# One operation and four small transfers for a head's hash bits, the product with the values in two runs, and a new order of the whole plan

## The chip, the cores and the metric

The kernel runs on one core of a Trainium2 chip. The metric is device time in microseconds (us), the median of the runs. TensorE (PE) multiplies matrices, VectorE (DVE), ScalarE (ACT) and GpSimd (POOL) work element by element, SyncE (SP) issues the transfers (DMAs). Each engine takes its instructions strictly in the order in which they stand in its own program, and waits on semaphores for what others make. SBUF is the on-chip memory, PSUM the memory that TensorE writes its sums to.

## The reference

Sixteen heads (2 batches of 8) of attention with 768 rows and 64 columns, masked by a hash, then two wide layers over 1536 tokens:

```python
q_bits = (np.einsum('bhsd,dk->bhsk', q, proj) > 0).astype(np.int64)   # 6 bits of a row
k_bits = (np.einsum('bhsd,dk->bhsk', k, proj) > 0).astype(np.int64)
mask = q_bucket[:, :, :, None] == k_bucket[:, :, None, :]             # all 6 bits alike
scores = np.where(mask, scale * np.matmul(q, k.transpose(0, 1, 3, 2)), -1e9)
attn = softmax(scores); x = np.matmul(attn, v)                        # heads side by side: 1536 x 512
h = x @ w_in1; x = (np.maximum(h, 0) + alpha * np.minimum(h, 0)) @ w_out1   # 512 -> 2048 -> 512
h = x @ w_in2; out = (P(h) / (Q(h) + 1e-6)) @ w_out2                        # P cubic, Q of |h| and h*h
```

## The kernel before, in words

**Precision.** Wide products are split: each operand is a rounded high part and a low rest, and three products (high by high, low by high, high by low) are summed. This is why `qh`, `ql`, `kx`, `k2`, `xh`, `xl`, `gh`, `gl`, `wih`, `wil`, `woh`, `wol` exist.

**A head.** `head(h)` loads the keys `rk` and queries `rq` (768 columns each), rounds them into `k2` and `qh` and takes the rests `kx` and `ql`. The matmuls `pb` (`bits_mm`, L420) project queries and keys on the six hash directions, with both signs, into one PSUM bank: four groups of 12 partitions (two column halves each of q and of k), which start at partitions 0, 32, 64 and 96. `bits_ev` (L425) turns one group into 0/1 numbers (for the keys 0 or a large penalty) and writes them to the rows 64 to 75 of `ql` (queries) or `k2` (keys). It runs four times a head, on DVE. By these rows the score product itself adds the penalty wherever the hashes differ.

**The six query tiles of a head.** For each tile of 128 queries: the scores `s` (four matmuls, L469 and L471, into two PSUM banks), the clamp `x` on DVE (L477), the exponential on ACT (L483), the transposition `t` on PE (L501, six blocks), the copy `pt` of the transposed tile to SBUF on ACT (L379). A little later, `mix(h)` multiplies the transposed weights with the values: `pv` (L559), six key tiles, in each two matmuls of 64 PE columns (the two query halves), which stand side by side in the array. `rb` (L532 and L539) brings the reciprocals of the row sums to the right partitions, and `over` on DVE (L565) scales `pv` into `acc`. The scores need all 128 PE columns, `pv` works in pieces of 64, `pb` in pieces of 32.

**The layers.** The 1536 tokens are four chunks (c = 0 to 3). A unit is one quarter of the 2048 inner columns for one chunk: four products `h` (L585), each followed by its activation on ACT, DVE and POOL, and then four (first layer) or three (second) products `o` (L601, L604). The first two units need batch 0 alone and stand among the heads 8 to 15; all others come after the last head. Weights arrive as raw 64-bit patterns and are taken apart on ACT and DVE (`mag`, `w`, `raw`, `wil`, `wol`; L271 to L305). The weights of the second layer are spilled to DRAM (`sp`) and loaded again.

**What sets the order.** `Plan` holds every step as a task with its costs on each engine that may do it, and `order()` runs a greedy list schedule before the program is written: of the tasks that could start soonest it takes the one with the highest `rank + bias`, and it chooses the engine that would finish first. `FAVOUR` holds for each kind of task the bias and factors on the costs by engine. The start times of this schedule are then the order in which the instructions are emitted, on each engine and on SP's one queue of transfers. `CAP` tells how many buffers each kind of tile has: two for `raw_qk`, so that a head's keys and queries each take the place of the head before. Six tasks `pv` per head, one for each key tile, are placed one by one:

```python
for kt in range(NT):
    plan.add("pv", pv(kt), {"pe": 0.68}, [bv["vr"], E[0][1], E[1][1]] + [bp] * bool(bp.writers), [bp], cols=1536)
```

Of the kernel before, what the change touches and what calls it, by code (L numbers as in the profile page):

```python
# [38 lines left out]
CAP = {"raw_qk": 2, "qh": 2, "kx": 2, "ql": 2, "k2": 2, "vr": 2,   # L39
# [20 lines left out]
    "w_load": (-113.1, {}), "w_abs": (-178.9, {}), "w_bits": (-42.2, {}),  # L60
    "w_hi": (0, {"dve": 1.27, "pool": 1.08, "act": 1.22}), "w_lo": (-69.2, {"pool": 0.5}), "load": (106.6, {}),
    "k2": (-79.6, {"act": 0.56, "pool": 0.46, "dve": 1.87}), "qh": (-74.9, {"dve": 0.2}), "kx": (12.9, {}),
    "ql": (0, {"pool": 0.85, "dve": 4.34}), "scores": (47.4, {}), "clamp": (253.6, {}), "flip": (-2, {}),
    "v_load": (-9.1, {}), "part1": (125.5, {"dve": 1.03, "pool": 0.87, "act": 0.54}),
    "part2": (31.5, {"dve": 78.83, "pool": 0.16}), "spread": (4.1, {}),
    "x_hi": (0, {"act": 16.64, "dve": 1.63, "pool": 0.96}), "x_lo": (44.3, {"dve": 3.39}), "g_neg": (11.1, {}),
    "g_both": (-11.8, {}), "g_hi": (0, {"act": 1.85, "dvp": 1.64}), "g_lo": (-9.5, {"dve": 5.4, "pool": 1.8}),
    "s2": (-35.4, {}), "o_ev": (128, {"dve": 1.27, "dvp": 1.2, "act": 0.94}), "u_load": (63.1, {}),
    "u_abs": (4.2, {}), "u_bits": (9.2, {}), "u_hi": (-19.1, {"act": 2.3, "pool": 3.49, "dve": 0.49}),
    "u_lo": (0, {"dve": 3.4, "pool": 2}), "f_lo": (203.3, {"pool": 1.7, "dve": 1.73}),  # L70
    "g_lo1": (-110.6, {"dve": 1.1, "pool": 0.63}), "s21": (-153.7, {}), "a_g": (58.1, {"pool": 0.82, "dve": 0.39}),
    "x_hi2": (-64.8, {"dve": 0.34, "act": 1.04, "pool": 1.91}), "bits_ev": (47.5, {}), "c_abs": (126, {}),
    "take": (0, {"dvp": 1.78, "act": 0.32}), "g_neg1": (-114.7, {}), "g_hi1": (-48, {"dvp": 1.85, "act": 0.43}),
    "x_lo2": (0, {"pool": 1.75, "dve": 3.12}), "c_prep": (24, {}), "expo": (-60.3, {}),
    "a_sum": (0, {"dve": 3, "pool": 0.94}), "a_exp": (122.5, {}),
    "c_hi": (-178.9, {"pool": 0.97, "act": 0.46, "dve": 1.24}), "swap": (-23.6, {}), "f_out": (-168.6, {}),
    "o_ev2": (0, {"dvp": 0.72, "act": 1.38}), "a_mul": (-3.7, {"dve": 0.7, "pool": 1.04}), "a_abs2": (1.3, {}),
    "g_lo2": (120.8, {"pool": 0.74}), "a_p0": (-213.8, {}), "g_hi2": (28.8, {"dvp": 0.8}), "s1": (-11.9, {}),
    "c_bits": (0.3, {}), "store": (-205.3, {}), "reload": (-17.7, {}), "c_lo": (116.2, {}), "c_load": (-24.3, {}),
# [847 lines left out]
```

## Time and profile before

| | us |
|---|---|
| median of 3 runs | 815.6 (813.73 to 815.83) |
| the profiled execution | 812.87 |
| its span, first to last instruction | 811.0 |
| busy in it: PE / DVE / ACT / POOL | 783.1 / 703.9 / 554.7 / 185.5 |
| TensorE's granted clock, mean | 0.999 |

The heads with the two early units fill about the first 290 us of the span, the first layer the stretch to about 550 us, the second layer the rest. Busy time of PE counts overlapping matmuls once, and their ends are modelled; what a step really takes on PE is read from one start to the next.

### The profile page before, as it was taken

Reading aid. Unit: us, or ns where it says so; the run is one execution under the profiler, and the core shown is the slowest. Engines: PE = TensorE matmul, PEld = TensorE weight load, DVE = VectorE, ACT = ScalarE, POOL = GpSimd, SP = SyncE. Lnnn points to the kernel's source line nnn. Section 1 sums busy time; section 2 is a strip of 40 time slices with the busy share of each in tenths; the row PEclk is TensorE's granted clock in tenths of the full one; section 3 lists DMA queues with packets and bytes.
Section 4 is the critical chain, followed back from the end, with each engine's and each line's share of the span. In section 5 each row is a group of like instructions: output and inputs, shape, how many; then the busy total and the mean of one; then the engine's idle time right before and its main releaser. Section 6 shows DMA issues by size and latency. Waiting matters only on the chain.

```text
span 811.0 us, 12442 instructions
## 1 busy us (share of the span) xinstructions
PE 783.1 (97%) x4416; PEld 667.2 (82%) x4416; DVE 703.9 (87%) x1369; ACT 554.7 (68%) x1074; POOL 185.5 (23%) x194
## 2 busy tenths in 40 slices
PE   4999999989999999999999999998999999999998
PEld 2676676667666779999999999997899998888986
DVE  5889989878677579898889889999999999989983
ACT  3978787766666645664445444599999888877870
POOL 3242432311230230000000000145434234432220
PEclk9999999999999999999999999999999999999999
DMA  5213222313110022335543465514222441140012
GB/s 189 97 60 104 85 86 81 108 38 110 44 59 1 27 79 79 104 104 176 170 136 102 124 203 160 203 54 156 61 97 61 149 155 58 61 143 2 13 53 91
DMA packets 25693, 78.67 MB, mean 97 GB/s; under 512 B 2976, under 2 KB 2976, under 8 KB 24096
## 3 DMA queue, kind: packets, MB, share of 16 engines
q1 hardware_dynamic: 25632, 77.88, 29.8%
q8 instruction: 35, 0.57, 0.3%
q14 instruction: 26, 0.21, 0.1%
HBM read 62.14 MB, written 15.73 MB: 96 GB/s over the span
## 4 chain that ended last, share of the span: by engine, by line
PE 72%; DVE 16%; ACT 6%; issue 3%; POOL 1%; DMA 1%; SPq 0%; DVEq 0%; POOLq 0%; ACTq 0%
PE h L585 23%; PE o L601 13%; PE o L604 9%; PE pv L559 8%; PE t L501 7%; PE s L469 5%; PE s L471 3%; DVE h L647 3%; PE h L601 2%; DVE gl L388 2%; DVE h L665 1%; DVE x L477 1%; PE pb L420 1%; DVE h L641 1%; DVE w L294 1%
## 5 line engine op out<-in xcount | busy, mean ns | idle before, releaser
L585 PE MATMUL h<-xh,wih 128*128 128x384 f32 x512 | 174.0, 340 | 6.6 <-DVE gl L388 4.9
L585 PE MATMUL h<-xl,wih 128*128 128x384 f32 x512 | 172.2, 336 | 0.0
L585 PE MATMUL h<-xh,wil 128*128 128x384 f32 x512 | 172.1, 336 | 0.0
L477 DVE TENSOR_SCALAR_CACHE_REDUCE x<-s 128x768 f32<-128x768 f32 x96 | 91.7, 956 | 32.1 <-PE s L471 28.3
L585 PEld LDWEIGHTS h<-xh,wih 128*128 128x128 f32 x512 | 96.1, 188 | 12.6 <-DVE gl L388 8.1
L483 ACT ACTIVATE x<-x,st 128x768 f32<-128x768 f32 x96 | 89.3, 931 | 16.6 <-DVE x L477 15.0
L379 ACT ACTIVATE pt<-t 128x768 f32<-128x768 f32 x96 | 77.0, 804 | 32.1 <-PE t L501 31.2
L650 POOL TENSOR_TENSOR al<-al,ap 128x384 f32<-128x384 f32 x64 | 67.8, 1060 | 133.5 <-DVE ap L650 62.2
L585 PEld LDWEIGHTS h<-xh,wil 128*128 128x128 f32 x512 | 96.2, 188 | 0.8
L585 PEld LDWEIGHTS h<-xl,wih 128*128 128x128 f32 x512 | 96.1, 188 | 0.0
L501 PEld LDWEIGHTS t<-eyes,x 128*128 128x128 f32 x576 | 64.1, 140 | 26.7 <-issue 12.2
L501 PE MATMUL t<-eyes,x 128*128 128x128 f32 x576 | 80.9, 277 | 1.3 <-ACT pt L379 0.4
L559 PE MATMUL pv<-pt,vr 128*64 128x384 f32 x384 | 78.1, 505 | 0.0
L604 PE MATMUL o<-woh,gl 128*128 128x512 f32 x192 | 75.5, 393 | 0.0
L604 PE MATMUL o<-wol,gh 128*128 128x512 f32 x192 | 75.5, 393 | 0.0
L604 PE MATMUL o<-woh,gh 128*128 128x512 f32 x192 | 75.4, 393 | 0.0
L601 PE MATMUL o<-gh,woh 128*128 128x384 f32 x224 | 75.4, 336 | 0.0
L601 PE MATMUL o<-gl,woh 128*128 128x384 f32 x224 | 75.3, 336 | 0.0
L601 PE MATMUL o<-gh,wol 128*128 128x384 f32 x224 | 75.3, 336 | 0.0
L388 DVE TENSOR_TENSOR gl<-h,gh 128x384 fp32r<-128x384 f32 x128 | 69.0, 550 | 5.8 <-PE h L585 4.3
L281 ACT ACTIVATE raw<-raw 128x512 uint32<-128x512 uint32 x64 | 43.1, 674 | 39.6 <-DMA raw<-w_in 18.4
L379 ACT ACTIVATE gh<-h 128x384 fp32r<-128x384 f32 x110 | 51.0, 489 | 27.4 <-DVE h L665 14.5
(104 smaller groups left out, 1641.2 us busy)
## 6 DMA issues: line engine op xcount, KB each, us to landing
raw<-w_in SPq DMA_DIRECT2D x32, 512.0 KB, 4.0
raw<-w_out SPq DMA_DIRECT2D x32, 512.0 KB, 4.1
rk<-kT SPq DMA_DIRECT2D x16, 384.0 KB, 3.1
rq<-qT SPq DMA_DIRECT2D x16, 384.0 KB, 3.9
sp<-w SPq DMA_DIRECT2D x24, 256.0 KB, 4.9
sp<-mag SPq DMA_DIRECT2D x24, 256.0 KB, 4.9
vr<-vN SPq DMA_DIRECT2D x8, 384.0 KB, 3.3
wih<-sp SPq DMA_DIRECT2D x3, 1024.0 KB, 4.8
```

The lines of the kernel that those rows point to most:

```text
L281: s_.activation(self.low, self.low, AF.Copy, scale=2.0 ** -9 * (1 - 2.0 ** -22))
L379: s_.activation(out, in_, AF.Copy, scale=scale)
L388: eng[e].tensor_tensor(out, a, b, op=ALU.subtract)
L469: te.matmul(sp[:, j, :HALF], K["qh"][:, q], K["kx"][:, j * HALF:(j + 1) * HALF], start=True, stop=False)
L477: v_.tensor_scalar(x.rearrange("p (j c) -> p j c", j=2), T["s"][:, :, :HALF], SCALE, FAR, op0=ALU.mult, op1=ALU.min, accum_out=T["st"])
L483: s_.activation(T["x"], T["x"], AF.Exp, bias=T["st"], scale=-1.0, accum_out=tr["ss"][:, tt, half:half + 1])
L501: te.transpose(o[:, c], T["x"][:, c], idf)
L559: te.matmul(T["pv"][64 * half:64 * half + 64, :HALF], tv["vr"][:, m, kt, :], E[half][0]["pt"][:, kt, :], start=(kt == 0), stop=(kt == NT - 1))
L585: te.matmul(o, wt[:, kc, f], xt[:, kc], start=(n == 0), stop=(n == 3 * KC - 1))
L601: te.matmul(op[:, :HALF], lt[:, m, d], rt, start=(n == 0), stop=(n == 3 * FT - 1))
L604: te.matmul(op[:, :], lt[:, d], rt[:, m], start=(n == 0), stop=(n == 3 * FT - 1))
L650: eng[e].tensor_tensor(P[a], P[a], P[b], op=op)
```

## The change

`bits_ev` becomes one DVE operation over all 128 partitions of the bank, into a new tile `bt` (two buffers). Two new tasks then move its four groups to the rows 64 to 75 of `ql` and `k2`, by two transfers each on SP's queue, 12 partitions by 384 numbers of four bytes (18 KB) a transfer; those to `k2` are held until `kx` is made, which reads `k2`. `pv` becomes two tasks of three key tiles. Some costs in the plan change (0.70 to 0.78 for `pb`, 0.34 to 0.36 for `rb`), and the whole table `FAVOUR` is another one, so that the order and the engines of nearly all steps are chosen anew.

```diff
+PVS = 2
 FAVOUR = {
-    "eye": (17.2, {}), "eye_prep": (47.4, {"act": 0.22, "dve": 2.47, "pool": 1.46}), "a_abs": (-37.2, {}),
+    "a_abs": (8.3, {"act": 3.26}), "a_abs2": (0, {"act": 9.87}), "a_exp": (330.6, {"act": 1.09}),
...
-        def bits_ev(n):
-            to, j, r = T["ql" if n < 2 else "k2"], n % 2, slice(32 * n, 32 * n + 2 * NB)
-            v_.tensor_scalar(to[64:64 + 2 * NB, j * HALF:(j + 1) * HALF], T["b"][r, :HALF],
-                             cst[r, 0:1], cst[r, 1:2], op0=ALU.is_ge, op1=ALU.mult)
+        def bits_ev(e):
+            T["bt"] = tl(hp, "bt", [128, HALF], F32R, f"bt{h}")
+            v_.tensor_scalar(T["bt"], T["b"][:, :HALF], cst[:, 0:1], cst[:, 1:2], op0=ALU.is_ge, op1=ALU.mult)
+
+        def move(n):
+            def f(e):
+                for j in range(2):
+                    r = 64 * n + 32 * j
+                    nc.sync.dma_start(out=T[("ql", "k2")[n]][64:64 + 2 * NB, j * HALF:(j + 1) * HALF].bitcast(F32),
+                                      in_=T["bt"][r:r + 2 * NB].bitcast(F32))
+            return f
...
-        for n in range(4):
-            plan.add("bits_ev", lambda e, n=n: bits_ev(n), {"dvp": 0.6}, [b, B["kx"], B["ql"]],
-                     [B["ql" if n < 2 else "k2"]])
+        bt = plan.buf("bt")
+        plan.add("bits_ev", bits_ev, {"dvp": 0.6}, [b], [bt])
+        for n in range(2):
+            plan.add("bits_mv", move(n), {"dma": 1.0}, [bt, *([B["kx"]] * n)], [B[("ql", "k2")[n]]])
...
-                for half in range(2):
-                    te.matmul(T["pv"][64 * half:64 * half + 64, :HALF], tv["vr"][:, m, kt, :],
-                              E[half][0]["pt"][:, kt, :], start=(kt == 0), stop=(kt == NT - 1))
+                for kt in range(part * NT // PVS, (part + 1) * NT // PVS):
+                    for half in range(2):
+                        te.matmul(T["pv"][64 * half:64 * half + 64, :HALF], tv["vr"][:, m, kt, :],
+                                  E[half][0]["pt"][:, kt, :], start=(kt == 0), stop=(kt == NT - 1))
...
-        for kt in range(NT):
-            plan.add("pv", pv(kt), {"pe": 0.68}, [bv["vr"], E[0][1], E[1][1]] + [bp] * bool(bp.writers), [bp], cols=1536)
+        for part in range(PVS):
+            plan.add("pv", pv(part), {"pe": 0.684 * NT / PVS + 0.17}, [bv["vr"], E[0][1], E[1][1]] + [bp] * bool(bp.writers), [bp], cols=1536 * NT // PVS)
```

The order on PE before, in the fourth head (`t` and `s` belong to tiles of that head and the next, `pv_710` is the product with the values of the head before):

```order
111 L501 MATMUL t_2_719<-eyes,x_2_663 128x128 x6
112 L469 MATMUL s_5_728<-kx_465,qh_491 128x384 x2
113 L471 MATMUL s_5_728<-k_447,ql_103 128x384 x2
114 L559 MATMUL pv_710<-pt_0_516,vr_142 64x384
115 L559 MATMUL pv_710<-pt_3_593,vr_142 64x384
116 L501 MATMUL t_3_744<-eyes,x_3_680 128x128 x6
117 L559 MATMUL pv_710<-pt_0_516,vr_142 64x384
118 L559 MATMUL pv_710<-pt_3_593,vr_142 64x384
119 L469 MATMUL s_0_756<-kx_597,qh_616 128x384 x2
120 L471 MATMUL s_0_756<-k_579,ql_102 128x384 x2
121 L559 MATMUL pv_710<-pt_0_516,vr_142 64x384
122 L559 MATMUL pv_710<-pt_3_593,vr_142 64x384
```

The order on PE in the change, where the same product stands (`pv_761`):

```order
110 L578 MATMUL pv_761<-pt_0_538,vr_154 64x384
111 L578 MATMUL pv_761<-pt_3_610,vr_154 64x384
112 L578 MATMUL pv_761<-pt_0_538,vr_154 64x384
113 L578 MATMUL pv_761<-pt_3_610,vr_154 64x384
114 L578 MATMUL pv_761<-pt_0_538,vr_154 64x384
115 L578 MATMUL pv_761<-pt_3_610,vr_154 64x384
116 L519 MATMUL t_3_782<-eyes,x_3_724 128x128 x6
117 L578 MATMUL pv_761<-pt_0_538,vr_154 64x384
118 L578 MATMUL pv_761<-pt_3_610,vr_154 64x384
119 L578 MATMUL pv_761<-pt_0_538,vr_154 64x384
120 L578 MATMUL pv_761<-pt_3_610,vr_154 64x384
121 L578 MATMUL pv_761<-pt_0_538,vr_154 64x384
```

Before, the pairs of `pv_710` are scattered: five runs in 21 rows, with transpositions and scores between them. In the change they stand in two runs of three pairs. Over all sixteen heads there are 73 runs of `pv` before and 31 in the change.

SP's queue before, around the loads of the sixth and seventh head (`rk`, `rq`):

```order
20 L408 DMA rk_734<-kT 128x768
21 L408 DMA rq_765<-qT 128x768
22 L408 DMA rk_875<-kT 128x768
23 L408 DMA rq_906<-qT 128x768
24 L271 DMA raw<-w_out 128x512
25 L452 DMA vr_984<-vN 128x768
```

SP's queue in the change, the same two heads:

```order
29 L418 DMA rk_752<-kT 128x768
30 L441 DMA ql_102<-bt_739 12x384 x2
31 L441 DMA k_614<-bt_739 12x384 x2
32 L418 DMA rq_777<-qT 128x768
33 L281 DMA raw<-w_out 128x512
34 L418 DMA rk_891<-kT 128x768
35 L441 DMA ql_103<-bt_889 12x384 x2
36 L441 DMA k_779<-bt_889 12x384 x2
37 L418 DMA rq_928<-qT 128x768
38 L281 DMA raw<-w_out 128x512
```

Between the load of the next head's keys and that of its queries there now stand the four transfers of a head's bits (`x2` is two of them), sixteen times in the program, 64 in all.

The end of the heads on PE before (`pv_2931` is the last head's product, L601 is an `o` of an early unit):

```order
683 L532 MATMUL rb_2954<-ident,rr_2906 12x128
684 L559 MATMUL pv_2931<-pt_0_2781,vr_2401 64x384
685 L559 MATMUL pv_2931<-pt_3_2871,vr_2401 64x384
686 L539 MATMUL rb_2954<-rt,sel 128x128 x3
687 L559 MATMUL pv_2931<-pt_0_2781,vr_2401 64x384
688 L559 MATMUL pv_2931<-pt_3_2871,vr_2401 64x384
689 L601 MATMUL h<-gh,woh_70 128x384
690 L601 MATMUL h<-gh,wol_71 128x384
```

The end of the heads on PE in the change (L604 is `h` of the third unit):

```order
729 L578 MATMUL pv_3021<-pt_3_2982,vr_2355 64x384
730 L557 MATMUL rb_3016<-rt,sel 128x128 x3
731 L578 MATMUL pv_3021<-pt_0_2897,vr_2355 64x384
732 L578 MATMUL pv_3021<-pt_3_2982,vr_2355 64x384
733 L578 MATMUL pv_3021<-pt_0_2897,vr_2355 64x384
734 L578 MATMUL pv_3021<-pt_3_2982,vr_2355 64x384
735 L578 MATMUL pv_3021<-pt_0_2897,vr_2355 64x384
736 L578 MATMUL pv_3021<-pt_3_2982,vr_2355 64x384
737 L604 MATMUL h<-xh_2971,wih_68 128x384
738 L604 MATMUL h<-xh_2971,wil_69 128x384
```

Before, matmuls of an early unit follow the last `pv`; in the change both early units stand ahead of the last scores, and after the last `pv` comes the third unit, which needs the last head's output.

## Rows read from the trace of the kernel before

**Rows 1.** The page, part 1: busy time, share of the span, instructions of each engine

```profile
PE 783.1 (97%) x4416; PEld 667.2 (82%) x4416; DVE 703.9 (87%) x1369; ACT 554.7 (68%) x1074; POOL 185.5 (23%) x194
```

**Rows 2.** Busy time of each engine in stretches (us, count), clock, DMA share, GB/s

```profile
20.00:160.00 140.00, 136.92 (x889) 91.10 (x888) 123.92 (x242) 112.29 (x207) 45.19 (x50) 1.00 0.29 90
160.00:180.00 20.00, 16.58 (x102) 13.36 (x100) 15.47 (x30) 13.00 (x27) 3.67 (x3) 1.00 0.09 27
180.00:280.00 100.00, 100.00 (x619) 69.16 (x616) 72.83 (x138) 67.97 (x125) 19.76 (x21) 1.00 0.16 51
280.00:300.00 20.00, 18.15 (x100) 14.18 (x100) 14.69 (x28) 7.18 (x14) 5.91 (x7) 1.00 0.25 80
...
540.00:560.00 20.00, 17.87 (x92) 15.91 (x91) 19.75 (x37) 18.83 (x39) 11.91 (x12) 1.00 0.46 168
```

**Rows 3.** TensorE in order of time: start, us, line, operation, tiles, count

```profile
44.97 0.84 PE L501 MATMUL t<-eyes,x 128*128 128x128 f32 x6
45.57 0.60 PE L469 MATMUL s<-kx,qh 128*128 128x384 f32 x2
...
46.35 0.82 PE L501 MATMUL t<-eyes,x 128*128 128x128 f32 x6
...
47.88 0.61 PE L469 MATMUL s<-kx,qh 128*128 128x384 f32 x2
...
48.77 0.87 PE L559 MATMUL pv<-pt,vr 128*64 128x384 f32 x4
49.57 0.87 PE L501 MATMUL t<-eyes,x 128*128 128x128 f32 x6
50.20 0.60 PE L469 MATMUL s<-kx,qh 128*128 128x384 f32 x2
...
51.07 1.51 PE L559 MATMUL pv<-pt,vr 128*64 128x384 f32 x8
52.52 0.87 PE L501 MATMUL t<-eyes,x 128*128 128x128 f32 x6
53.32 0.54 PE L559 MATMUL pv<-pt,vr 128*64 128x384 f32 x2
```

**Rows 4.** Chain of work that ended last, around 141 us: start, us, what

```profile
141.21 3.38 PE pv L559 x20
```

**Rows 5.** Who waited for whom: us in total, times, longest

```profile
ACT pt L379 <- PE t L501: 31.2, 39, 2.2
...
DVE x L477 <- PE s L471: 28.3, 37, 1.7
```

**Rows 6.** Groups by line: busy us, mean ns of one, idle before, releaser

```profile
L388 POOL TENSOR_TENSOR ql<-qh,rq 64x768 fp32r<-64x768 f32 x16 | 33.0, 2065 | 19.8 <-DVE qh L383 11.4 <-ACT qh L379 7.7
...
L650 DVE TENSOR_TENSOR ap<-ap,t 128x384 f32<-128x384 f32 x39 | 22.4, 574 | 1.0 <-ACT t L653 0.9
L425 DVE TENSOR_SCALAR k<-pb,every 12x384 fp32r<-12x384 f32 x32 | 21.8, 681 | 0.9
L425 DVE TENSOR_SCALAR ql<-pb,every 12x384 fp32r<-12x384 f32 x32 | 21.4, 670 | 2.2 <-PE pb L420 1.2
...
L383 DVE COPY rs<-rb 128x384 f32<-128x384 f32 x8 | 4.4, 556 | 0.5
```

**Rows 7.** DMA issues by line: count, KB each, median us to landing

```profile
rk<-kT SPq DMA_DIRECT2D x16, 384.0 KB, 3.1
...
wil<-sp SPq DMA_DIRECT2D x3, 1024.0 KB, 6.9
...
out<-acc SPq DMA_DIRECT2D x12, 256.0 KB, 2.0
```

**Rows 8.** SyncE in order of time: two loads issued one behind the other

```profile
48.02 0.33 SPq L408 DMA_DIRECT2D rk<-kT  x1
48.44 0.38 SPq L408 DMA_DIRECT2D rq<-qT  x1
```

**Rows 9.** TensorE at the start of the first head, in order of time

```profile
13.19 1.32 PE L471 MATMUL s<-k,ql 128*128 128x384 f32 x2 [2.97 <-DVE k L425]
```

More of the change, by code (lines that the diff above doesn't have):

```diff
@@ L36 @@
 MAG_MAX = float(np.uint32(0x47EFFFFF).view(np.float32))
-CAP = {"raw_qk": 2, "qh": 2, "kx": 2, "ql": 2, "k2": 2, "vr": 2,
+CAP = {"raw_qk": 2, "qh": 2, "kx": 2, "ql": 2, "k2": 2, "bt": 2, "vr": 2,
        "s": 2, "b": 1, "pv": 1, "x": 5, "st": 8, "ss": 4, "pt": 4, "rr": 2, "rt": 1, "rs": 1,
@@ L58 @@
 FAVOUR = {
-    "eye": (17.2, {}), "eye_prep": (47.4, {"act": 0.22, "dve": 2.47, "pool": 1.46}), "a_abs": (-37.2, {}),
[L60 to L79, printed above, removed]
@@ L80 @@
-    "o_add1": (-59.7, {}), "back": (25.7, {}), "a_quad": (15.9, {}), "f_abs": (-50.9, {}), "a_sq": (-9.5, {}),
-    "scaled": (34.5, {"dvp": 0.78, "act": 1}), "s22": (-23.1, {}), "w_tail": (-102.2, {}), "a_log": (42.9, {}),
+    "a_abs": (8.3, {"act": 3.26}), "a_abs2": (0, {"act": 9.87}), "a_exp": (330.6, {"act": 1.09}),
+    "a_g": (307.8, {"dvp": 2.74}), "a_log": (331.4, {}), "a_mul": (0, {"dve": 0.33}), "a_n1": (121.4, {"dvp": 1.1}),
+    "a_n2": (187.3, {"dvp": 1.1}), "a_p0": (-74.9, {}), "a_p1": (11.5, {"act": 1.6}),
@@ new lines @@
+    "a_prep": (0.9, {"dve": 25.03}), "a_quad": (14.4, {"dvp": 0.49}), "a_sq": (-4.8, {"act": 3.06}),
+    "a_sum": (5.5, {}), "back": (0.4, {"act": 3.87}), "bits": (0.1, {"pe": 1.14}), "bits_ev": (65.3, {"dvp": 1.12}),
+    "c_abs": (95.2, {"act": 0.4}), "c_bits": (26.2, {"dve": 1.53}),
+    "c_hi": (1.9, {"act": 0.01, "dve": 10.69, "pool": 0.08}), "c_lo": (125.7, {"dve": 0.71}),
+    "c_load": (46.6, {"dma": 0.54}), "c_prep": (52.4, {}), "c_tail": (30.5, {"act": 1.82}),
+    "clamp": (93.7, {"dvp": 2.24}), "expo": (-0.6, {"act": 1.21}), "eye": (-92.4, {}),
@@ new lines @@
+    "eye_prep": (-76.1, {"act": 0.48, "dve": 0.84, "pool": 2.3}), "f_abs": (-257.9, {}),
+    "f_bits": (32.9, {"dve": 0.68}), "f_lo": (3.6, {"dve": 0.39}), "f_load": (0.2, {"dma": 2.24}),
+    "f_out": (-79.2, {}), "f_tail": (198.6, {}), "flip": (150.1, {}), "g_both": (-117, {"dvp": 0.9}),
+    "g_both1": (-105.7, {"dvp": 0.17}), "g_hi": (-18.1, {"act": 0.01, "dvp": 0.17}),
+    "g_hi1": (21.3, {"act": 0.65, "dvp": 19.62}), "g_hi2": (58.6, {"dvp": 25777.3}), "g_lo": (-109, {"dvp": 0.43}),
+    "g_lo1": (-1.1, {"dvp": 1.64}), "g_lo2": (84.4, {}), "g_neg": (0, {"act": 0.46}), "g_neg1": (2.8, {}),
@@ new lines @@
+    "guard": (14, {"dve": 0.65}), "k2": (1.5, {"act": 0.01, "dve": 0.2, "pool": 0.3}), "kx": (-13.7, {}),
+    "load": (59.6, {"dma": 1.87}), "o_add1": (-169, {}), "o_add2": (0.2, {"dvp": 2.92}),
+    "o_ev": (0, {"act": 1.41, "dvp": 0.95}), "o_ev2": (10.4, {"dvp": 4.3}), "over": (-1.9, {}),
+    "part1": (-65.7, {"act": 5.7, "pool": 0.53}), "part2": (85.1, {"pool": 1.88}), "pv": (0, {"pe": 0.52}),
+    "qh": (-206.4, {"act": 0.41, "dve": 0.04, "pool": 0.07}), "ql": (-1.7, {"dve": 0.32, "pool": 0.49}),
@@ new lines @@
+    "recip": (106.2, {}), "reload": (-12.4, {"dma": 3.42}), "s1": (0, {"pe": 0.43}), "s11": (13.3, {}),
+    "s12": (0, {"pe": 0.12}), "s2": (2.7, {}), "s21": (1.6, {"pe": 1.48}), "s22": (-93.1, {"pe": 1.35}),
+    "scaled": (4, {"act": 0.02, "dvp": 0.33}), "spread": (76.4, {"pe": 0.25}), "store": (0, {"dma": 0.06}),
+    "swap": (-36.2, {"none": 0.58}), "take": (464.4, {"dvp": 1.85}), "turn": (103.6, {"pe": 3.79}),
+    "u_abs": (9.3, {}), "u_bits": (145.8, {"dve": 0.22}), "u_hi": (-77.1, {"act": 0.88, "dve": 0.02, "pool": 1.07}),
@@ new lines @@
+    "u_lo": (89.7, {"dve": 0.41}), "u_load": (10.9, {"dma": 4.51}), "u_tail": (30.4, {"act": 2.07}),
+    "v_load": (29.4, {}), "w_abs": (-11.9, {"act": 0.62}), "w_bits": (-56.4, {}),
+    "w_hi": (-124.6, {"act": 0.94, "pool": 0.4}), "w_lo": (-101.8, {"dve": 3.14}), "w_load": (160.7, {"dma": 0.39}),
+    "w_tail": (0, {"act": 3.69}), "x_hi": (-11.5, {"act": 0.13, "dve": 34.42, "pool": 0.65}),
+    "x_hi2": (13.6, {"act": 0.05, "dve": 0.36, "pool": 0.33}), "x_lo": (-102, {"dve": 0.53, "pool": 0.36}),
@@ L82 @@
+    "x_lo2": (-433.4, {}),
 }
@@ L439, in head @@
         b = plan.buf("b")
-        plan.add("bits", bits_mm, {"pe": 0.7}, [*R, BZ], [b], cols=1536)
-        for n in range(4):
-            plan.add("bits_ev", lambda e, n=n: bits_ev(n), {"dvp": 0.6}, [b, B["kx"], B["ql"]],
-                     [B["ql" if n < 2 else "k2"]])
+        plan.add("bits", bits_mm, {"pe": 0.78}, [*R, BZ], [b], cols=1536)
+        bt = plan.buf("bt")
+        plan.add("bits_ev", bits_ev, {"dvp": 0.6}, [b], [bt])
+        for n in range(2):
+            plan.add("bits_mv", move(n), {"dma": 1.0}, [bt, *([B["kx"]] * n)], [B[("ql", "k2")[n]]])
         return T, B
@@ L550, in mix, with pv @@
         plan.add("back", back, {"dvp": 0.2, "act": 0.16}, [bb], [brt])
-        plan.add("spread", spread, {"pe": 0.34}, [brt], [bb], cols=36)
+        plan.add("spread", spread, {"pe": 0.36}, [brt], [bb], cols=36)
         plan.add("scaled", scaled, {"act": 0.41, "dvp": 0.47}, [bb], [brs])
-        def pv(kt):
+        def pv(part):
             def f(e):
@@ L853, in swap_rest @@
         more(o=ps2, h2=ps2, g2h=mp, g2l=mp, mag2=mp, w322=mp, ap=mp, al=mp, aq=mp)
-    for f, b, tags in ((swap, BS[2], ("raw_qk", "qh", "kx", "ql", "k2")),
+    for f, b, tags in ((swap, BS[2], ("raw_qk", "qh", "kx", "ql", "k2", "bt")),
                        (swap_rest, BS[3], ("x", "pt", "vr", "st", "ss", "rr", "rt", "rs", "s", "b", "pv", "h"))):
```

## The prediction

> **What bounds the kernel now.** I read the page's busy line first. PE is busy 783.1 of 811.0 us, DVE 703.9, ACT 554.7 [rows 1]. These are averages, so the second view was busy time by stretch: PE is busy 136.9 of 140 us from 20 to 160, and all of 180 to 280, where DVE is busy 73% and ACT 68% of the time [rows 2]. The reader is to see that PE leaves gaps in three places alone, 3.4 us in 160 to 180, 1.9 in 280 to 300 and 2.1 in 540 to 560, besides the start; the granted clock is 1.00 in all of them. Third came the waits: the clamp on DVE waits 28.3 us for scores, the copy on ACT 31.2 us for transpositions [rows 5]. The helpers wait for PE. So what counts in the heads is how long PE takes for its row of tasks. That is read from starts, not from busy time: one task's cost is the distance to the start of the next.
>
> **Fewer runs of `pv`.** In the rows of PE, scores followed by a transposition take 0.78 us (45.57 to 46.35), a transposition followed by scores 0.60 (44.97 to 45.57). A single pair-set of `pv` (one key tile) takes 0.80 (48.77 to 49.57), two in a row 1.45 (51.07 to 52.52) [rows 3], five in a row 3.38 [rows 4]. So a further key tile costs 0.65, and the start of a run 0.15. The neighbours pay too: scores ahead of `pv` take 0.89 and 0.87 (47.88 to 48.77, 50.20 to 51.07), 0.10 more than 0.78; a transposition behind `pv` takes 0.63, 0.03 more than 0.60; one between two runs takes 0.80 (52.52 to 53.32), which leaves 0.17 for standing ahead of one [rows 3]. A run thus costs 0.15 + 0.10 to 0.17 + 0.03, that is 0.28 to 0.35 us, and I take 0.32. The two orders hold 73 runs before and 31 in the change, 42 fewer: 13.4 us of PE time (11.8 to 14.7). Heads 1 to 8 give 17 of them (32 to 15), 5.4 us; heads 9 to 16 give 25 (41 to 16), 8.0 us. Matmul counts don't change. In the later heads PE is without a gap and DVE and ACT are at 73% and 68%, so I count the 8.0 in full.
>
> **DVE in the first eight heads.** There DVE is busy 123.9 of 140 us, 88% [rows 2], and it must keep up with a shorter PE row. Leaving: 40 of the old bit operations lie in this stretch, at 0.68 us [rows 6], 27 us. Coming: eight `bt` operations. Before shows none of 128 partitions; the bounds are 0.56 (the copy `rs` of the same 384 columns out of the same bank) and 0.68 (12 partitions) [rows 6], and I take 0.68, since it is the same operation: 5.4 us. Three of the rests `ql` come over from GpSimd in about these heads: twice a 384-column operation of 0.57 [rows 6], 3.4 us. Two more weight pieces are converted here than before, six operations each, by the same 0.57 some 7 us. Sum: 123.9 - 27 + 5.4 + 3.4 + 7 = 112.7 in a stretch of 140 - 5.4 = 134.6 us, 84%. It fits, a little looser than before, but in runs of 2.1 us of `pv` DVE gets no new scores. For gaps from this I charge 1.5 us (0 to 5.4, the whole gain of these heads). The other moves (28 sums `al` from GpSimd to DVE at 0.57, 14 rounding copies from DVE to ACT) roughly cancel in the layers, where both orders give PE the same matmuls: 0.
>
> **The transfers.** Before, the fourth bit operation of a head was written straight to its rows. Now, from the end of `pb`: the operation 0.68, four issues on SP 0.42 apart (48.02 to 48.44 [rows 8]), so the last goes out 1.3 later, and it lands 2.0 to 3.1 later by the nearest rows, 256 KB out and 384 KB in [rows 7]. That is 4.0 to 5.1 us, 6.1 if DVE is in the middle of a clamp. What PE has to do between `pb` and the first scores that need the bits is, in the new order, with the costs above: in the fifth head two scores, two transpositions, the two runs of `pv` at 2.10 and a matmul `rb`, 7.3 us; in the second head 5.5, on the mean of heads 2 to 10 6.7, from the eleventh on over 10 because early-unit products stand there. So the transfers are hidden, by 0.6 to 2.7 us; for the second head and some late ones I charge 1 us in all. On SP's queue the four stand behind the next head's keys, which wait for the same `pb`, and hold back the next head's queries by 1.7 us; those are needed only a head later. If the cover is gone, each head waits for the difference. At the very start PE already waits 2.97 us for the last bit operation [rows 9]; now it waits there for the transfers. One operation instead of four against 3.3 to 4.4 us of issue and landing: 0, with 1.5 either way.
>
> The Trainium skill, "DMA: Bandwidth & Descriptors" (Rules for kernel authors), speaks against this part: many small transfers should be made one large one, since under 64 KB one pays mostly overhead, with a fixed part of about 2.0 us each. The trace has 2.0 us too, for 256 KB. If the fixed parts overlap, as the issues 0.42 us apart suggest, an estimate by that page gives 2.04 us for 18 KB and the same sum; if they queue up, it is the slower rival below.
>
> **The end of the heads.** Before, products of an early unit cover the chain behind the last scores, and still 280 to 300 leaves 1.9 us [rows 2]. In the change nothing stands between the last transposition, the two runs of `pv` and the third unit, which needs the last head's output. PE then sees the copy ahead of `pv` and the scaling, rounding and rest behind it, four operations of 0.56 to 0.8 us, partly beside earlier matmuls of `h`: 3 us against 1.9, so +1 (-2 to +3).
>
> **Sum.** The profiled execution took 812.9. Minus 13.4, plus 1.5, plus 1, plus 1: 803. The median of the runs shown is 2.7 above this execution, so 805.7; I say 805.
>
> **Rivals.**
> *Slower: the bits come late.* Place: the first scores of heads 2 to 10. If the four transfers take their 2.0 us one after another, or stand behind the 384 KB of keys issued just ahead, the last lands at 0.68 + 4 x 2.0 = 8.7 us, or, by the slowest landing in the trace (6.9 [rows 7]), at 8.9. Against 6.7 that is 2.0 to 2.2 us in nine heads, 18 to 20 us: 824. It decides from 1.5 us a head on, when the landing takes some 5.5 us. For it: each keys' load stands directly ahead. Against: 18 KB, and loads of 384 KB that land in 3.1. This is also what the skill's rule would make of it. Chance 0.15.
> *No change: the scattered key tiles filled gaps.* If PE, after a run of 2.1 us, must wait for the clamp or the copy as long as it saved, all 13.4 is given back: 816. For it: DVE at 88% in the first heads. Against: rows 5, and 180 to 280 with idle helpers. Chance 0.13.
> *Half of it: DVE becomes the bound in the first eight heads alone,* and 5.4 is lost: 811. Chance 0.12.
> *Better:* the new order also closes the gaps at 160 to 180, 280 to 300 and 540 to 560, 7.4 us together, of which most would go: 798. The three lie where DVE or GpSimd held PE up, and GpSimd loses ten of its sixteen `ql` at 2.07 us [rows 6]. Chance 0.10.
>
> **How the numbers follow.** My forecast, 799 to 810, has 0.50. The time is its centre, 805. About 0.3% (2.4 us) is what a measurement of this kernel can tell from no change: the forecast, the better case and the half case are all faster, 0.72; the no-change case 0.13; slower 0.15. The range leaves out the slow rival's upper part and the extreme of the better one: 795 to 818.
>
> **What would show it.** Right: PE's distance from a `pv` start to the next other task 2.1 us for three key tiles, about 31 such runs, and the last clamp some 10 us earlier than before while both early units are done; PE without gaps from 180 to 280. The old line L425 is one group of 16 at 0.56 to 0.7 us. The transfers show a landing near 2 us, and the scores' second half does not wait on them beyond the second head. Wrong: a wait of scores for a DMA of over 1.5 us in each early head; or DVE over 95% busy between 20 and 150 with PE waiting for the clamp; or the stretch of the two layers longer than before by several us, because the new table placed their steps worse, which I count as nothing.

## The result and the profile after

| | before | after |
|---|---|---|
| median | 814.66 us (4 runs, 813.65 to 815.83) | 807.04 us (4 runs, 806.57 to 809.89) |
| profiled execution, span | 812.87, 811.0 | 809.89, 808.0 |
| ratio after / before, of the means | | 0.9913, 95% interval 0.9884 to 0.9942 |

The change makes the kernel 7.6 us faster, where 10.6 were forecast. The same kernel beside later experiments gave 806.92 us and 0.9918 (0.9898 to 0.9938). The profiled execution of after is the slowest of its four, and that of before is faster than the four in its column, so the two traces differ by 3 us only. Beside the later experiments the median of before was 812.85 to 813.39 us; beside the repeated change the gain is 6.5 us.

Busy time of each engine, against [rows 1]:

```profile
PE 775.9 (96%) x4416; PEld 672.8 (83%) x4416; DVE 677.2 (84%) x1358; ACT 565.5 (70%) x1087; POOL 120.7 (15%) x144
```

PE is busy 7.2 us less with as many matmuls, DVE 26.7 less, POOL 64.8 less. Busy time by stretch of after, against [rows 2]:

```profile
20.00:160.00 140.00, 136.77 (x915) 96.68 (x915) 118.33 (x252) 116.67 (x207) 31.02 (x40) 1.00 0.32 100
160.00:180.00 20.00, 19.49 (x125) 14.89 (x124) 10.81 (x23) 12.30 (x24) 1.24 (x3) 1.00 0.22 64
180.00:280.00 100.00, 96.31 (x603) 75.08 (x602) 55.48 (x117) 59.27 (x105) 3.92 (x10) 0.98 0.11 32
280.00:300.00 20.00, 15.87 (x94) 11.66 (x93) 16.93 (x37) 14.29 (x28) 1.60 (x2) 1.00 0.26 79
...
540.00:560.00 20.00, 19.24 (x97) 16.92 (x96) 19.80 (x39) 18.61 (x39) 12.02 (x14) 1.00 0.43 158
```

PE's gaps have moved: 160 to 180 is nearly closed (3.4 to 0.5), 540 to 560 too (2.1 to 0.8). New gaps stand in 180 to 280, where before had none (3.7), and in 280 to 300 (1.9 to 4.1).

A run of `pv`, in the chain of waits of after (start, us, what; x12 are three key tiles):

```profile
254.98 2.09 PE pv L578 x12
257.07 0.55 PE s L487 x2
```

That is 0.15 + 3 x 0.65 = 2.10 as forecast. The bits, as instructions on their tile (ns shortest, median, longest, first and last start), and who waited for them and for PE in the whole span:

```profile
L441 SPq DMA_DIRECT2D ql<-bt x32: 722/750/1091, 11.0 to 255.1; - x32
L441 SPq DMA_DIRECT2D k<-bt x32: 713/714/1325, 12.7 to 256.7; - x32
L435 DVE TENSOR_SCALAR bt<-pb,every x16: 664/676/708, 10.3 to 253.5; 128x384 fp32r<-128x384 f32 x16
```

```profile
ACT pt L389 <- PE t L519: 44.2, 44, 1.9
...
DVE x L495 <- PE s L489: 31.1, 30, 2.9
...
PE s L489 <- DMA k<-bt: 3.6, 1, 3.6
```

The operation over 128 partitions takes what one over 12 took. PE waits for a transfer of bits once, in the first head. SP, however, needs a median of 0.71 to 0.75 us for each; the forecast set the issues 0.42 apart, as loads are.

The end of the heads on PE after (start, us, line, what, idle before and releaser):

```profile
290.41 2.16 PE L578 MATMUL pv<-pt,vr 128*64 128x384 f32 x12
294.13 0.45 PE L604 MATMUL h<-xh,wih 128*128 128x384 f32 x1 [1.56 <-ACT rs L389]
```

and the third unit's first matmul before:

```profile
298.07 0.33 PE L585 MATMUL h<-xh,wih 128*128 128x384 f32 x1
```

Everything ahead of this point is the same PE work in both orders. Before (first line) and after, in the columns of [rows 2]:

```profile
0.00:298.07 298.07, 278.87 (x1729) 191.28 (x1729) 238.53 (x461) 206.58 (x380) 79.21 (x92) 1.00 0.25 79
0.00:294.13 294.13, 270.45 (x1729) 197.19 (x1729) 207.63 (x437) 205.60 (x363) 42.59 (x67) 0.99 0.26 81
```

It ends 3.9 us earlier in this trace (4.6 in the repeated one, at 293.51 with PE busy 270.27). PE is busy 8.4 to 8.6 us less up to there, and idle 4.0 to 4.5 us more (19.2 us before, 23.7 and 23.2 after). From there to the end it is 513.9 us after and 512.9 before (512.7 in the repeated one): the gain lies in the heads.

### The profile page after: what moved, and what is told of

It reads as the page before. It is cut to its first block, busy times and chain, and to the rows that moved or that the text cites. A ratio compares the mean times of both kernels' runs of the same rounds, so it can differ in the third digit from the quotient of the medians.

```text
span 808.0 us, 12525 instructions
## 1 busy us (share of the span) xinstructions
PE 775.9 (96%) x4416; PEld 672.8 (83%) x4416; DVE 677.2 (84%) x1358; ACT 565.5 (70%) x1087; POOL 120.7 (15%) x144
## 4 chain that ended last, share of the span: by engine, by line
PE 61%; DVE 19%; ACT 10%; issue 4%; DMA 4%; SPq 1%; POOL 0%; DVEq 0%; ACTq 0%; POOLq 0%
PE h L604 20%; PE o L620 10%; PE o L623 9%; PE pv L578 6%; PE t L519 5%; PE s L487 4%; PE s L489 3%; DVE h L666 2%; DMA rq<-qT 2%; PE h L620 2%; DVE gl L398 2%; DVE x L495 2%; PE pb L430 2%; ACT al L657 1%; ACT ap L657 1%
## 5 line engine op out<-in xcount | busy, mean ns | idle before, releaser
L604 PE MATMUL h<-xh,wih 128*128 128x384 f32 x512 | 174.3, 340 | 6.2 <-DVE gl L398 4.0
L604 PE MATMUL h<-xl,wih 128*128 128x384 f32 x512 | 172.3, 336 | 0.2 <-DVE xl L398 0.2
L604 PE MATMUL h<-xh,wil 128*128 128x384 f32 x512 | 172.0, 336 | 0.0
L604 PEld LDWEIGHTS h<-xh,wih 128*128 128x128 f32 x512 | 96.1, 188 | 12.8 <-DVE gl L398 8.1
L604 PEld LDWEIGHTS h<-xh,wil 128*128 128x128 f32 x512 | 96.2, 188 | 0.8
L604 PEld LDWEIGHTS h<-xl,wih 128*128 128x128 f32 x512 | 96.1, 188 | 0.5 <-DVE xl L398 0.5
L519 PEld LDWEIGHTS t<-eyes,x 128*128 128x128 f32 x576 | 67.2, 142 | 15.0 <-issue 3.0
L389 ACT ACTIVATE gh<-h 128x384 fp32r<-128x384 f32 x124 | 57.6, 491 | 27.6 <-DVE h L684 13.2
L578 PE MATMUL pv<-pt,vr 128*64 128x384 f32 x384 | 68.8, 494 | 0.0
L291 ACT ACTIVATE raw<-raw 128x512 uint32<-128x512 uint32 x64 | 43.1, 674 | 35.2 <-DMA raw<-w_in 16.9
L730 DVE TENSOR_TENSOR acc<-acc,o 128x384 f32<-128x384 f32 (+1 forms) x84 | 50.5, 605 | 18.1 <-PE o L620 9.0
```

The lines of the kernel that those rows point to most:

```text
L291: s_.activation(self.low, self.low, AF.Copy, scale=2.0 ** -9 * (1 - 2.0 ** -22))
L389: s_.activation(out, in_, AF.Copy, scale=scale)
L519: te.transpose(o[:, c], T["x"][:, c], idf)
L604: te.matmul(o, wt[:, kc, f], xt[:, kc], start=(n == 0), stop=(n == 3 * KC - 1))
L730: v_.tensor_tensor(a, a, o, op=ALU.subtract if moe else ALU.add)
```

## Experiments

A ratio is to the kernel before beside it. The first four split the change into its parts.

**e1: only the product regrouped.** The order of before, with each head's `pv` brought together into two runs.

```diff
+    for n in range(0, len(pvs), NT // 2):
+        last = pvs[n + NT // 2 - 1]
+        for t in pvs[n:n + NT // 2 - 1]:
+            seq.remove(t)
+            seq.insert(seq.index(last), t)
```

> The kernel before with its own order on every engine; only, in each head, the first two of each three key tiles of pv are moved down to stand directly ahead of the third: 31 runs of pv instead of 73, four bit operations as before. Theory (a run's start costs PE about 0.3 us and PE bounds the heads): 12 us less than before, some of it given back to new waits, 803 to 806. Rival (scattered key tiles fill time in which PE would wait anyway): 813 to 816. Second rival (what the change gains is the DVE operations it saves): 813 to 816 too, since none is saved here.

816.07 us, 1.0038 (1.0023 to 1.0053): some 3 us slower. Its stretches, to be read against [rows 2]:

```profile
20.00:160.00 140.00, 133.75 (x888) 94.90 (x887) 126.33 (x242) 112.01 (x208) 44.23 (x50) 0.99 0.29 91
280.00:300.00 20.00, 17.29 (x89) 12.33 (x88) 15.52 (x33) 6.57 (x14) 2.96 (x5) 0.91 0.21 68
```

DVE rises to 90% and PE stands idle 6.3 us in the first stretch, where it stood 3.1 before. By the waits, PE's matmuls `s` wait 4.9 us in 8 places for the clamp, against 1.7 in 2. The granted clock falls as well, to 0.91 in the second row. The scattered key tiles had been the filling. The theory of fewer runs, taken alone, falls.

**e2: the change without its one operation.** Its order, but the four operations of before in place of `bt` and the transfers.

```diff
-                    nc.sync.dma_start(out=T[("ql", "k2")[n]][64:64 + 2 * NB, ...], in_=T["bt"][r:r + 2 * NB])
+                    v_.tensor_scalar(T[("ql", "k2")[n]][64:64 + 2 * NB, ...], T["b"][r, :HALF],
+                                     cst[r, 0:1], cst[r, 1:2], op0=ALU.is_ge, op1=ALU.mult)
```

> The changed kernel with its order kept, but the bits of a head are written again by four DVE operations of 12 partitions each, at the places of the transfers; no transfers. DVE gets 48 operations of 0.68 us back, 33 us, half of them in the first eight heads. If the saved DVE time matters: DVE reaches some 95% there, PE waits for clamps, 811 to 814. If it does not, and only the runs of pv count: 805 to 808, the lower end if the start gains from it.

826.73 us, 1.0167 (1.0147 to 1.0187), some 20 us above the change, far more than expected:

```profile
20.00:160.00 140.00, 123.17 (x793) 86.25 (x793) 126.79 (x253) 104.37 (x185) 25.63 (x33) 0.96 0.26 85
```

DVE stands at 91% of this stretch, close to e1, but here PE is idle for 16.8 us of it (3.2 in the change) and the granted clock falls to 0.96. Over the whole span PE waits 17.3 us for DVE's clamps and `rr`, against 5.9 in the change. The 48 operations more cost 48 x 0.68 = 33 us of DVE, and in this order, which was not planned for them, over half of it lands on PE.

**e3: the change with the old table.** Only `FAVOUR` goes back (neither table has an entry for the transfers, and the old one has none for `pv`).

```diff
 FAVOUR = {
-    "a_abs": (8.3, {"act": 3.26}), "a_abs2": (0, {"act": 9.87}), "a_exp": (330.6, {"act": 1.09}),
+    "eye": (17.2, {}), "eye_prep": (47.4, {"act": 0.22, "dve": 2.47, "pool": 1.46}), "a_abs": (-37.2, {}),
...
```

> The changed kernel with the table FAVOUR of the kernel before; the order is planned anew with it, 31 runs of pv. If the new table matters little: 805 to 809. If the table has to fit its tasks: the runs still save 12 us of PE time, but the gaps grow, 810 to 818.

834.33 us, 1.0268 (1.0253 to 1.0284):

```profile
20.00:160.00 140.00, 128.87 (x840) 90.77 (x839) 105.39 (x217) 108.44 (x200) 40.30 (x47) 0.99 0.30 94
...
560.00:800.00 240.00, 231.73 (x1147) 209.78 (x1146) 220.27 (x427) 206.20 (x418) 86.11 (x85) 0.97 0.23 81
```

In the first stretch PE is idle 11.1 us with DVE at 75%: it is the order, not DVE's load. And the layers are slower too, 525.0 us from the third unit's first matmul to the end where before took 512.9. So no part gains alone or in these pairs: +0.4% (runs), +1.7% (runs and table), +2.7% (runs and bits), and -0.9% all three. The table alone, the bits alone and the table with the bits were not run.

**e4: sixteen runs more.** The change, with the first run of each head split over the next tasks of PE: 47 runs for 31, all else in place.

```diff
+    for first, second in zip(pvs[::2], pvs[1::2]):
+        i, k = seq.index(first), seq.index(second)
+        gaps = [n for n in range(i + 1, k) if seq[n].eng == "pe"]
+        cuts = ([n + 1 for n in gaps] + [k, k])[:2]
...
```

> The changed kernel with its order kept; only, in each head the second and third key tile of the first run of pv are moved behind the next and the next but one step on TensorE: 47 runs of pv instead of 31, the same matmuls. If each run's start costs 0.3 us where PE is the bound: 16 x 0.32 = 5 us more, 811 to 813. If short pieces help as fillers: 805 to 807.

811.26 us, 0.9973 (0.9959 to 0.9987). Against the change's 0.9913 and 0.9918 that is 4.5 to 4.9 us, 0.28 to 0.31 a run. By the intervals, about 2 us either way, 0.16 to 0.42 would fit. In the traces less of it shows: up to the third unit PE is busy 272.8 us here and 270.3 in e5, 0.16 us a run, or up to 0.26 with the low clock of e5, which did not come here (1.7 us at most, see e5). So a run has a price where the others can follow, and these are the bounds of it.

The other eight look for what was given back, and for a better kernel.

**e5: the change again,** unaltered.

> The changed kernel itself, beside the three others of this comparison. All theories: 0.990 to 0.993 of the kernel before, 805 to 808 us. Of the profile: if the granted clock of 0.91 between 240 and 260 us belongs to the order of the tasks there, it is seen again; if it was a chance of that execution, it is not, and the waits between 180 and 260 us fall by about 6 us.

806.92 us, 0.9918 (0.9898 to 0.9938). The low clock is there again. Four microseconds each of after (first fence) and e5 (second):

```profile
248.00:252.00 4.00, 2.61 (x11) 2.26 (x10) 3.30 (x7) 2.10 (x4) 0.00 (x0) 0.71 0.00 0
252.00:256.00 4.00, 4.00 (x27) 2.10 (x28) 1.65 (x3) 2.71 (x5) 0.00 (x0) 0.86 0.02 5
```

```profile
248.00:252.00 4.00, 3.13 (x14) 2.63 (x18) 2.71 (x6) 2.25 (x5) 0.00 (x0) 0.61 0.00 0
252.00:256.00 4.00, 4.00 (x30) 2.12 (x22) 1.64 (x3) 3.16 (x6) 0.00 (x0) 0.97 0.04 9
```

PE stands idle 2.0 us from 244 to 252 in both, waiting for the clamp up to 1.39 us at a time, and the clock falls. By these rows that is worth at most 1.7 us (0.29 x 4 + 0.14 x 4 in after). In e7 it fell there too (0.90 from 244 to 252, 2.1 us idle); in e4, e6, e9, e10 and e12 it stayed at 1.00, with 2.0 to 2.2 us idle as well. What decides it was not found.

**e6: no transfers for the first head.**

```diff
+            if h == 0:
+                for n in range(4):
+                    r = slice(32 * n, 32 * n + 2 * NB)
+                    v_.tensor_scalar(T[("ql", "k2")[n // 2]][64:64 + 2 * NB, ...], T["b"][r, :HALF], ...)
+                return
```

> The changed kernel, with the bits of the first head alone written by four operations of VectorE and no transfers for that head. Theory that the first head waits for its transfers (TensorE's first matmul of scores at 14.85 us waits 3.64 us for the transfer k<-bt): that wait goes, the first matmul comes 1.6 to 3.6 us earlier, and the kernel takes that much less, 803.5 to 805.5 us. Rival, that the start hangs on VectorE (the first clamp stands behind a conversion of weights and two operations of the next head, and came at 18.19 us): the first matmul comes earlier, the first clamp does not or comes later by the two or three operations more (some 1 us), and the time stays, 807 to 808 us.

810.47 us, 0.9955 (0.9939 to 0.9971): slower by 3 to 3.5. PE's wait of 3.6 us for the transfers became one of 1.3 us for DVE, yet DVE came to the first clamp only here (17.65 in e5):

```profile
19.52 0.96 DVE L501 TENSOR_SCALAR_CACHE_REDUCE x<-s 128x768 f32<-128x768 f32 x1
```

Three operations more on DVE, 2 us, and the second head's scores (head 1 in the expectations) start 3.0 us later than in e5, at 28.53. Of that, 0.4 us is the first load, which landed later in this execution; and PE waited 4.3 us for the first tile's exponential, with the lower clock behind that wait. The start hangs on DVE; the largest wait of PE was not its bound.

**e7: two output products moved into the gap at the end of the heads.**

```diff
+    held = early + [t for t in seq if t.kind == "o_ev" and any(d in early for d in t.deps)]
...
+    seq[at:at] = held      # early: the last two s2 ahead of the last pv; at: directly behind it
```

> The changed kernel, with the last two output projections of the early units taken from their place among the last heads' tasks and put directly behind the last product with the values, where TensorE stands idle some 4.5 us before the third unit's feed-forward. Theory that this idle time is a hole that any ready work fills: 2 to 4 us less, 803 to 805 us. Rival, that the two projections cover waits of about the same size where they stand now: no change, 806 to 808 us; or that their evictions delay the third unit's own chain on VectorE and ScalarE: up to 2 us more.

809.80 us, 0.9951 (0.9937 to 0.9965): some 3 us slower than the change.

```profile
296.11 0.34 PE L604 MATMUL h<-xh,wih 128*128 128x384 f32 x1
...
299.11 0.44 PE L604 MATMUL h<-xh,wih 128*128 128x384 f32 x1 [1.28 <-ACT xh L389]
```

They fill the gap, but with 4.2 us of products taken out ahead of it, the last `pv` came only 1.0 us earlier than in e5: where they had stood they had covered waits of nearly their size. Their evictions then held back the third unit's `xh`.

**e8: every transfer twice.** The bits are written again with the same values.

```diff
+                    nc.sync.dma_start(out=T[("ql", "k2")[n]][64:64 + 2 * NB, ...], in_=T["bt"][r:r + 2 * NB])
```

> The changed kernel, with every one of the four transfers of bits issued twice (eight a head; the second writes the same bits again), nothing else changed. One issue took 0.72 us of SyncE, so the bits land some 2.9 us later in every head. Theory that the transfers land ahead of need by 1.5 to 3 us after the first head: the start later by 2.9 us, 0 to 1.4 us for each of the next six heads, 810 to 815 us. If the bits had far more room than that (as they would if nothing but the first head hangs on them): 809 to 811 us. If they have none and each head of the first eight already hangs on the transfer: 8 x 2.9 = 23 us more, about 830 us.

926.70 us, 1.1389 (1.1365 to 1.1414). My size of the edit was wrong, as SP shows (one head):

```profile
52.44 0.76 SPq L441 DMA_DIRECT2D ql<-bt  x1
54.91 0.72 SPq L443 DMA_DIRECT2D ql<-bt  x1
...
61.22 0.72 SPq L441 DMA_DIRECT2D k<-bt  x1
63.23 0.72 SPq L443 DMA_DIRECT2D k<-bt  x1
```

and PE's first scores of the head, which need the bits:

```profile
62.56 0.66 PE L491 MATMUL s<-k,ql 128*128 128x384 f32 x1 [4.07 <-DMA k<-bt]
65.24 0.69 PE L491 MATMUL s<-k,ql 128*128 128x384 f32 x1 [2.02 <-DMA k<-bt]
```

The second write of the same bytes waits for the first to land: 2.47 us from issue to issue for the first transfer of this head, 2.0 for the other three, and the scores follow 2.0 us behind the last issue. A head's transfers hold SP 11.5 us (52.44 to 63.95) instead of 3.6. PE waits 6.1 us for them in this head, so some 1.8 of the 7.9 us more were room. Each head became 7.5 us longer on average (119.8 / 16), part of it by the granted clock, which was 0.85 from 20 to 160. The run also gives the landing that after did not show. In after, the same head's first and last issue and its scores:

```profile
49.26 1.53 SPq L441 DMA_DIRECT2D ql<-bt  x2
...
51.60 1.28 SPq L441 DMA_DIRECT2D k<-bt  x1
...
55.76 0.51 PE L489 MATMUL s<-k,ql 128*128 128x384 f32 x2
```

With 2.0 us the last has landed at 53.6, or at 54.2 if this issue, 0.57 us longer than most, lands that much later: 1.6 to 2.2 us ahead of the scores. Over heads 2 to 10 the scores start 2.8 to 4.6 us behind the last issue (least in the second head, 23.75 to 26.56), so the room is 0.8 to 2.6 us.

**e9: three operations ahead of the weight pieces at the end of the heads.** Only places in the order change here and in e10 and e12 (e11 starts from e6).

```diff
+    moves = [(spread, [scaled]), (last_pv, [over_0, over_1])]   # in words: behind the first, the others
```

> The changed kernel with three operations earlier at the end of the heads: ScalarE's copy rs and VectorE's two products acc<-pv,rs of the last head stand ahead of the pieces of weight preparation that they stood behind. In the changed kernel TensorE is done with the last product with the values at 291.95 us and waits 1.56 us for rs, which waits behind a conversion wih that waits for VectorE. Theory that the end of the heads hangs on this place in the queues, not on too little ready work: the third unit starts 1.5 us earlier, and the kernel takes 1.5 to 2 us less, 805 to 805.5 us (ratio 0.989 to 0.990). Rival, that the weight preparation that is now later is what the layers wait for: no change or up to 1 us more.

808.75 us, 0.9950 (0.9931 to 0.9968):

```profile
290.45 0.44 PE L604 MATMUL h<-xh,wih 128*128 128x384 f32 x1
...
295.19 0.69 PE L604 MATMUL h<-xh,wih 128*128 128x384 f32 x1 [2.88 <-ACT xh L389]
295.68 0.52 PE L604 MATMUL h<-xh,wil 128*128 128x384 f32 x1
```

The third unit starts 3.1 us earlier than in e5 and stops after nine matmuls, and the next nine run at the lower clock (1.2 GHz: 0.52 us for 0.34, a start every 0.32 us for 0.17 to 0.18). From 295 to 299 the granted clock is 0.59. The span is the same, 806.2 us.

**e10: the first clamps ahead of the next head's work at the start.**

```diff
+    moves = [(clamp_0, [qh]), (clamp_1, [kx, bits_ev]), (clamp_2, bits[0:2]), (clamp_3, bits[2:4]), ...]   # in words
```

> The changed kernel with nothing added or taken away, only the order of the start changed: the first two clamps stand ahead of the next head's kx and of the second piece of weights on VectorE, whose operations follow by twos behind the next clamps; the two operations of ScalarE that belong to them move with them. The transfers of the first head stay. Theory that the start hangs on VectorE's order (first clamp at 17.65 us, though its matmuls were done by about 15.5): the first clamp comes some 2 us earlier, head 1 starts 1.5 to 2 us earlier, 805 to 805.5 us (0.989 to 0.990). Rival, that the time is given back in the next heads, where VectorE has no room for the weight pieces: 0.991 to 0.993.

809.24 us, 0.9950 (0.9934 to 0.9967). DVE and POOL of this kernel:

```profile
15.71 0.96 DVE L495 TENSOR_SCALAR_CACHE_REDUCE x<-s 128x768 f32<-128x768 f32 x1 [2.02 <-PE s L489]
...
18.48 1.94 DVE L422 SCALAR_TENSOR_TENSOR kx<-k,low,rk 128x768 fp32r<-128x768 f32 x1
```

```profile
17.77 1.83 POOL L398 TENSOR_TENSOR ql<-qh,rq 64x768 fp32r<-64x768 f32 x1 [5.09 <-DVE qh L393]
```

The clamp did come 1.9 us earlier. Then `kx`, 1.02 us in e5, fell beside POOL's `ql` and took 1.94, the third clamp came as late as ever (20.93 us, 21.04 in e5), and the second head's scores started 0.9 us later.

**e11: e6 with the clamps ahead of both weight pieces.**

> The changed kernel with the first head's bits written by four operations of VectorE (as in the kernel e6, 810.5 us) and the first two clamps ahead of both pieces of weights. Theory that e6 lost because the first clamp stood behind 2 us more of VectorE's work, not because the transfers cost nothing: the first clamp comes at some 13.5 us instead of 19.5 in e6, head 1 starts 3 to 5 us earlier than in e6 and 1 to 2 us earlier than in the changed kernel, 804.5 to 806 us (0.988 to 0.990). Rival, that the four operations cost their 2 us on VectorE wherever they stand: 808 to 810 us (0.993 to 0.996).

818.84 us, 1.0063 (1.0044 to 1.0082). The first clamp came at 13.51 as expected, but the edit broke something else. ScalarE in order of time:

```profile
27.45 0.65 ACT L291 ACTIVATE raw<-raw 128x512 uint32<-128x512 uint32 x1 [10.11 <-DMA raw<-w_in]
```

The late weight piece kept its buffer, the next weights could not be loaded, and ScalarE stood 10 us with the copies `pt` behind that instruction. So this run says nothing on the four operations.

**e12: e9, with the last head's `xh` and `xl` moved up as well.**

```diff
+    moves = [(spread, [scaled]), (last_pv, [over_0, x_hi, over_1, x_lo])]   # in words
```

> As e9, and besides ScalarE's first copy xh and VectorE's difference xl of the last head stand directly behind the product acc<-pv,rs that they need, ahead of the weight pieces. In e9 the third unit started 3.06 us earlier than in the changed kernel beside it, but TensorE then waited 2.88 us for this xh and the granted clock fell to 1.2 GHz for 3 us behind that wait (0.52 us a matmul instead of 0.34, eleven of them: 2.0 us). Theory that the gain of e9 was lost in this wait: the xh comes 1.8 us earlier, the wait shrinks from 2.88 to about 1 us, the clock stays, and the kernel takes 2 to 4 us less than e9 and 1 to 3 us less than the changed kernel: ratio 0.988 to 0.991. Rival, that the weight pieces now later stop the layers by as much: as e9, 0.992 to 0.997.

808.52 us, 0.9929 (0.9911 to 0.9947): by the intervals not to be told from e9, and not better than the change.

```profile
292.00 0.45 PE L604 MATMUL h<-xh,wih 128*128 128x384 f32 x1 [0.60 <-ACT xh L389]
...
302.25 0.69 PE L604 MATMUL h<-xh,wih 128*128 128x384 f32 x1 [2.81 <-DVE gl L398]
```

```profile
300.00:310.00 10.00, 7.75 (x36) 7.76 (x37) 10.00 (x22) 6.69 (x13) 0.00 (x0) 0.83 0.32 106
```

The wait for `xh` shrank from 2.88 to 0.60 and came back ten microseconds later as 2.81 for `gl`, again with a fall of the clock. DVE is busy 10.0 of these 10 us, and 17.7 of the 20 ahead of them, most of it with weight pieces (in the change it is 10.0 and 16.9). So by the traces the end of the heads hangs on DVE's total work there, and e9 and e12 only chose where PE meets it; no run took work off DVE there.

## Why the prediction was right, and where not

- **Fewer runs, -13.4.** Only a part of it is seen. The start of a run costs what was forecast: the steps of `pv`, from one start to the next, sum to 73.1 us before and 66.7 after, 6.4 less, close to 42 x 0.15 = 6.3. The rest of the price, 0.13 to 0.20 for the neighbours, does not show in the same way: PE's whole row up to the third unit is 8.4 to 8.6 us shorter, 10.3 at most with the low clock taken out, 0.20 to 0.25 a run for 0.32. The medians of e4 (0.28 to 0.31) are too wide to decide it. That the 8.0 of the later heads count "in full", and the sign "PE without gaps from 180 to 280", were wrong: that stretch has 3.7 us of gaps. PE waits for the clamp there, with DVE at 55% on average. A helper that is idle on average was taken for one that is never late.
- **DVE in the first heads, +1.5.** 112.7 us of 134.6 was forecast, 84%; 118.3 of 140 came, 85%; PE's gaps there grew by 0.2. (The sum took out the bits of ten heads and put in those of eight; the stretch has ten `bt`, so it is 114.1.) What the term did not say is how much hangs on it: e2 puts the saved DVE work at 20 us, more than the runs. The gain on PE is the runs' price, and in this order the DVE work is what lets it be kept.
- **Transfers, +1 and hidden.** Hidden, by 0.8 to 2.6 us in heads 2 to 10, as forecast (0.6 to 2.7); PE waits for them in the first head alone, so the 1 us charged was not needed. The two parts were off: the issues are some 0.78 apart and not 0.42, so in the head measured the bits land 5.2 to 5.7 us after `pb`'s end (48.44) and not 4.0 to 5.1; and PE's lead there was 7.3 us, above the mean of 6.7. The slow rival (824) did not come. By the Trainium skill, "DMA: Bandwidth & Descriptors" (Rules for kernel authors), small transfers pay mostly overhead: the trace agrees, with 2.0 us for 18 KB, but the overhead cost nothing where the order had 7 us of work beside it.
- **Start, 0.** The second head's scores start 0.6 to 1.1 us later. PE's wait for the transfers, 3.6 us, was not the cause: without them (e6) it became worse.
- **End of the heads, +1.** The gap grew by 2.3. The mechanism named, the chain behind the last `pv`, is there, but under it, as e9 and e12 are read, lies DVE's load of weight pieces.
- **Layers, 0.** +1.0 and -0.2 in two traces. Right.
- **The sign "last clamp some 10 us earlier"** was wrong: it comes at 283.52 us and came at 273.60. The forecast itself said that the early units now stand ahead of the last scores and not behind them; the third unit's start was the mark to name.
- **Not in the sum.** The gaps at 160 to 180 and 540 to 560 closed but for 1.3 us, 4.3 us in all: the better rival's mechanism, which counted 7.4. But its third gap, at 280 to 300, grew, and closing the one at 540 to 560 made the layers no shorter. Nor did DVE or GpSimd hold PE up in all three before: at 280 to 300 it was ACT (`rt` 0.69, `acc` 0.58 twice).

For the heads the sum forecast 13.4 less 3.5, that is 9.9 us; the third unit starts 3.9 us earlier (4.6 in e5). Two terms were mis-sized: PE's row is 8.4 to 8.6 us shorter and not 13.4, and PE is idle 4.0 to 4.5 us more where 3.5 were charged. The lower clock, which no term had, has a part in the first (1.7 us at most).

That 805 came so near 807.04 is partly luck. On the profiled executions 803 was forecast, and 809.89 and, repeated, 807.99 came. The forecast then added 2.7 us for the median of the first three runs of before, 815.6; later medians of before lie 2 to 3 us lower. Executions of the changed kernel lie between 806.22 and 809.89 us, and what their 3 to 4 us consist of was not settled. Nor was it shown which entries of the table matter, since it was only exchanged whole, or what the new table would gain with the old 73 runs.

## What to carry to other kernels

Price a regrouping from starts, and then ask who must keep up: here the shorter row on TensorE became a gain only together with 33 us of operations taken from VectorE and a new order, and each part that was tried without the others lost. Don't repair the largest visible wait of a planned order on its own: none of six such repairs gained, and most lost about 3 us (the medians tell about 2): where it was followed, the wait stood for an engine's backlog and came back a little later. Before a step is moved past others, look at what it holds (a buffer, a queue) and at what will then run beside it.
